# Float64 weights converted in pairs of chunks, with the low part formed on VectorE

## The chip, the cores and the metric

The kernel runs on one core of a Trainium2 chip. The metric is the time of one execution on the device, in microseconds (us); the median of several runs counts. The engines are TensorE (PE: matmuls, PEld: its weight loads), VectorE (DVE), ScalarE (ACT), GpSimd (POOL) and SyncE (SP), which issues all DMAs here. Each engine works through its own queue in order and waits at an instruction until what it needs is done.

## The reference

Attention with a window of 128 keys over 4 sequences of 576 tokens, 8 heads of 64, then two feed-forward networks (FFNs) over all 2304 tokens:

```python
scores = where(mask, scale * q @ k.T + bias, -1e9)      # causal, the last 128 keys
x = softmax(scores) @ v                                  # 2304 x 512
h = x @ w_in                                             # 512 -> 2048
x = (h * sigmoid(1.702 * h)) @ w_out                     # 2048 -> 512
g = x @ w_gate                                           # 512 -> 1536
out = (g * sigmoid(g) * (x @ w_val)) @ w_out2            # 1536 -> 512
```

q, k and v are float32. The five weight matrices are handed to the kernel as float64, and the kernel has to turn them into float32 itself.

## The kernel before

**Products.** Every float32 operand of an FFN product is split into hi + lo, two numbers of the type fp32r, and a product is three matmuls: hi by hi, hi by lo, lo by hi (`three`, L388 to L390). So weights, too, are needed as a hi and a lo part.

**Weights.** A chunk is 128 rows of 512 float64 numbers, 4 KB in each of the 128 partitions. The first FFN has 32 chunks (w_in and w_out in turn), the second 36 (w_gate, w_val, w_out2 in turn). `load_w` (L129) brings a chunk as pairs of 32-bit words into a slot of 4 KB; `split_w` (L135) turns it into float32 bit by bit and into hi and lo, which are written back into the same slot as the tile wt. It works in three steps. ScalarE rescales the upper words into the tile cv (L143). VectorE takes the sign (L145), joins it with the lower word's bits (L146) and joins both with the exponent and mantissa (L149). ScalarE copies the result to hi (L154), and GpSimd subtracts hi from it to make lo (L155). cv has three slots of one chunk.

**Slots.** The pool w has 32 slots, one for each chunk of the first FFN. Until a slot's chunk is loaded, block 0's queries, keys and values and the probabilities of blocks 0 and 1 lie in some of them (L95, L235, L236, L288, L312, L340). The second FFN's chunks come into four slots of their own (NX) and then into the slots of w in order, as the first FFN's last block has used the chunk in them.

**Order of work.** The first FFN and the attention go through the tokens in five blocks of 4, 3, 4, 3 and 4 tiles of 128 tokens. For each part f of the hidden layer, `h_part` makes the first product, ScalarE and VectorE apply the activation and the split into gh and gl (L409 to L414), and `y_part` makes the second product. `y_part` comes two parts after its `h_part` in the program (AHEAD). The attention of block 0 comes first, with an order written out by hand (`manual_schedule`, L555), into which the conversion of the first four chunks is put head by head (SPLITS0). The attention of the blocks after it lies in the gaps between the products of the block before. The order of the rest on each engine is set by a scheduler, which takes the program's order as priority, and which may run work earlier when its engine is free by its own estimate. So the first FFN's chunks are converted while block 0 goes through it, and the second FFN's while the last block does (L622 to L630). The second FFN goes through blocks of 4, 4, 4, 4 and 2 tiles, with `gv_part` and `o_part`; its split of the next block's input (L464) is on GpSimd.

**GpSimd's other work:** the probabilities' scaling (L269), the masks on transposed probabilities (L350, L353), and one of the two subtractions of a head's queries and keys (L204 for block 1, L208 for the others).

Of the kernel before, what the change touches and what calls it, by code (L numbers as in the profile page):

```python
# [8 lines left out]
F32 = mybir.dt.float32  # L9
F32R = mybir.dt.float32r  # L10
# [9 lines left out]
# how many parts of the hidden layers the first product of an FFN runs ahead of the second  # L20
AHEAD = 2
# parts of the first FFN's hidden layer that block 0 does before block 1, the rest after it
F0 = 10
# chunks of the second FFN's weights with slots of their own
NX = 4
# blocks of the first FFN and of the attention, in tiles of 128 tokens
A_BLOCKS = (4, 3, 4, 3, 4)
B_BLOCKS = (4, 4, 4, 4, 2)
# block 0's attention, in heads after a head's scores: its normalisation, transposes and values
NORM0, TRANSPOSE0, VALUES0 = 0.6, 2.2, 5.0  # L30
# heads of block 0 whose probabilities VectorE takes apart; ScalarE and GpSimd do the others
ON_VECTOR = (0, 2, 5)
# heads at which the splits of the first weight chunks begin, a head between their steps
SPLITS0 = (7, 8, 9, 10)
# the other blocks' attention: its share of the time, and lags in gaps between the FFN's products
SPREAD, SPLIT_LAG, TRANSPOSE_LAG, VALUES_LAG = 0.65, 0.3, 4.0, 3.0
# (1023 - 127) / 8 less in the upper eight bits of a float64's exponent
# [4 lines left out]
def attention_two_ffn(ctx: ExitStack, tc: tile.TileContext, q, k, v, w_in, w_out, w_gate, w_val, w_out2, yscr, out):  # L42
    """q, k: [H * D, tokens]; v: [H, 128, tiles, D]; w_in, w_gate, w_val: [F/128, 128, 512] and
    w_out, w_out2: [F, 512] as the bits of float64; yscr: [128, 4, tokens]; out: [tokens, 512].

    Every float32 operand of a product is split exactly into hi + lo with 12 significant
    bits each (float32r), so that single-pass products carry float32's accuracy."""
# [9 lines left out]
    NW1 = 2 * NF1  # L57
    NW2 = 3 * NF2
# [8 lines left out]
    # tiles of 128 tokens that go through the first and through the second FFN together, and,  # L67
    # for each block of the first, through the attention
# [6 lines left out]
    const = ctx.enter_context(tc.tile_pool(name="const", bufs=1))  # L75
    wpool = ctx.enter_context(tc.tile_pool(name="w", bufs=1, reuse_waits="tile"))
    cvp = ctx.enter_context(tc.tile_pool(name="cv", bufs=3))
# [13 lines left out]
    def constants():  # L91
        make_identity(nc, ident)
        # column j stands for the key at j in the query's tile up to the query's own position,
        # and beyond it for the key at j in the tile before: rel = key position - query position
        rel = wpool.tile([P, P], F32, tag=f"w{NW1 - 12}", name="rel")  # L95
        nc.gpsimd.iota(rel, pattern=[[1, P]], base=0, channel_multiplier=-1, allow_small_or_imprecise_dtypes=True)
        nc.vector.tensor_scalar(out=later, in0=rel, scalar1=0.0, scalar2=None, op0=ALU.is_gt)
        nc.vector.scalar_tensor_tensor(
            out=rel, in0=later, scalar=-float(WINDOW), in1=rel, op0=ALU.mult, op1=ALU.add
        )  # L100
        for h in range(H):
            # in units of unscaled scores
            slope = 2.0 ** (-8.0 * (h + 1) / H) / SCALE
            nc.vector.tensor_scalar(out=bias[:, h, :], in0=rel, scalar1=slope, scalar2=None, op0=ALU.mult)
        nc.vector.memset(never, -BIG)
        nc.vector.memset(drop, 1.0)
        nc.vector.memset(keep, 1.0)
# [21 lines left out]
    def load_w(pool, tag, src):  # L129
        """A chunk of float64 weights, as pairs of words, into the slot that its split will take."""  # L130
        t = pool.tile([P, 512, 2], U32, tag=tag, name="wraw")
        nc.sync.dma_start(out=t.rearrange("p c w -> p (c w)"), in_=src.bitcast(U32))
        return t, pool, tag

    def split_w(raw):  # L135
        """float64 -> float32 bit by bit (float32 has no exponents from 2^128, and those below 2^-119 go to zero),
        then hi + lo. In three steps."""
        words, pool, tag = raw
        low, high = words[:, :, 0], words[:, :, 1]
        c = cvp.tile([P, 512], U32, tag="cv", name="cv")  # L140
# [12 lines left out]
        t = pool.tile([P, 2, 512], F32R, tag=tag, name="wt")  # L153
        nc.scalar.activation(out=t[:, 0, :], in_=cf, func=AF.Copy)  # L154
        nc.gpsimd.tensor_tensor(out=t[:, 1, :], in0=cf, in1=t[:, 0, :].bitcast(F32), op=ALU.subtract)  # L155
        yield t

    def w1_src(i):
        f = i // 2
        return w_in[f] if i % 2 == 0 else w_out[f * P : (f + 1) * P, :]  # L160

    def w2_src(i):
        f = i // 3
        return (w_gate[f], w_val[f], w_out2[f * P : (f + 1) * P, :])[i % 3]

# [1 line left out]
    units = {}  # L167

    def span(j):
# [11 lines left out]
    def load_head(j, h):  # L181
        """Queries and keys, in both halves of the partitions."""
# [12 lines left out]
    def split_head(j, h):  # L195
        """Queries as hi over lo, keys as hi over hi and lo over lo: two products give all four parts."""
# [16 lines left out]
    def fold(i0, kinds, sb):  # L213
        """Puts the scores with the keys of the tile before into the places of the keys after the query."""
# [19 lines left out]
    # first slots of weights still to come that hold the probabilities of the first two blocks  # L234
    PROBS = (NW1 - 12, NW1 - 12)  # L235
    PFS = (NW1 - 20, NW1 - 8)  # L236
# [41 lines left out]
    def scores(j, h):  # L278
# [7 lines left out]
        else:  # L286
            if e == 0:
                u["probs"] = wpool.tile([P, 2, 4, P], F32, tag=f"w{PROBS[j] + h // 2}", name="probs")  # L288
            prob = u["probs"][:, e]
# [22 lines left out]
    def load_full(hp):  # L312
        """The first block's queries, keys and values, in slots of weights still to come: the queries of
        two heads, each head's keys with zeros in the other's place."""
        t0, n, _ = span(0)
        m = n * P
        qv = wpool.tile([P, 2, 512], F32, tag=f"w{NW1 - 8 + 2 * hp}", name="qv")
        kz = wpool.tile([P, 2, 512], F32, tag=f"w{NW1 - 7 + 2 * hp}", name="kz")
# [10 lines left out]
    def transposes(j, h):  # L329
        """A head's probabilities, keys on the partitions, apart by the tile of the key:  # L330
        before(0) own(0) before(1) own(1) ..."""
# [7 lines left out]
        else:  # L339
            pf = wpool.tile([P, 4, 2, P], F32, tag=f"w{PFS[j] + h}", name="pf")  # L340
# [3 lines left out]
        # of column q, partition k: the tile before for k > q, the query's own for k <= q  # L344
# [13 lines left out]
    def values(j, hp):  # L358
        """The outputs of two heads, which share TensorE's columns, by the tile of the keys."""
# [37 lines left out]
    def h_part(j, f):  # L397
# [3 lines left out]
        w = w1[2 * f]  # L401
# [6 lines left out]
        # x * sigmoid(1.702 x) = (1 + tanh(0.851 x)) * x / 2; the half is taken at the output  # L408
# [8 lines left out]
    def y_part(j, f):  # L417
# [7 lines left out]
        w = w1[2 * f + 1]  # L425
# [40 lines left out]
    def gv_part(b, f):  # L466
# [4 lines left out]
        for dst, w in ((pg, w2[3 * f]), (pv, w2[3 * f + 1])):  # L471
# [15 lines left out]
    def o_part(b, f):  # L487
# [4 lines left out]
        w = w2[3 * f + 2]  # L492
# [46 lines left out]
    load_w1(NW1 - 20)  # L539
# [18 lines left out]
    load_w1(8)  # L558
# [6 lines left out]
    def hooks(j, length):  # L565
        """The attention of block j, as (position, work) over the 2 * length gaps before its first FFN."""
# [37 lines left out]
    for idx, (j, f) in enumerate(seq):  # L604
        if (j, f) == (1, 0):
            load_w1(NW1)
        if j < 2:
            need = 2 * f + 3
            if j == 1:
                need = max(need, 2 * F0 + (2 * (NF1 - F0) * (f + 1)) // NF1)  # L610
# [11 lines left out]
        if j == na - 1:  # L622
            if f < KD:
                split_y(0, f, y2a)
            load_w2(NX if f == 0 else 2)
            split_next(w2, raw2, 2 * f - 4)
# [60 lines left out]
```

## Time and profile before

| | |
|---|---|
| median of 3 runs | 1008.58 us (1008.13 to 1009.61) |
| span of the profiled execution, first to last instruction | 1006.5 us |
| TensorE matmul busy | 964.8 us (96%) |
| VectorE busy | 528.1 us (52%) |
| ScalarE busy | 383.3 us (38%) |
| GpSimd busy | 265.2 us (26%) |
| bytes moved by DMA | 77.43 MB |

A row of the time line has an instruction's start, its length, the engine, the line of the kernel, the operation and its tiles (output<-input) with their shapes. A row of a group of instructions has their count (x), their busy time, the mean length of one in ns, and the idle time of the engine just before them. The rows of one engine overlap a little where the end of one is still under way as the next starts. Matmul ends are modelled, so TensorE's busy share says less than the number of its matmuls in a stretch.

### The profile page before, as it was taken

Reading aid. Unit: us, or ns where it says so; the run is one execution under the profiler, and the core shown is the slowest. Engines: PE = TensorE matmul, PEld = TensorE weight load, DVE = VectorE, ACT = ScalarE, POOL = GpSimd, SP = SyncE. Lnnn points to the kernel's source line nnn. Section 1 sums busy time; section 2 is a strip of 40 time slices with the busy share of each in tenths; the row PEclk is TensorE's granted clock in tenths of the full one; section 3 lists DMA queues with packets and bytes.
Section 4 is the critical chain, followed back from the end, with each engine's and each line's share of the span. In section 5 each row is a group of like instructions: output and inputs, shape, how many; then the busy total and the mean of one; then the engine's idle time right before and its main releaser. Section 6 shows DMA issues by size and latency. Waiting matters only on the chain.

```text
span 1006.5 us, 13342 instructions
## 1 busy us (share of the span) xinstructions
PE 964.8 (96%) x4792; PEld 804.3 (80%) x4792; DVE 528.1 (52%) x1138; ACT 383.3 (38%) x889; POOL 265.2 (26%) x327
## 2 busy tenths in 40 slices
PE   7887979999999999999888999999999999999998
PEld 5566669997878789998666788888888888888897
DVE  7899996564555345637999822232223222322232
ACT  4577753564444345635555521121121112111121
POOL 4756552363133125623444510100020001000000
PEclk9898999999999999999999999999999999999999
DMA  9824440132232113226444210010001000100010
GB/s 306 268 87 145 141 142 23 49 112 87 65 103 71 51 41 110 61 74 241 177 167 147 84 42 1 21 63 1 0 27 48 1 1 11 42 0 1 1 43 22
DMA packets 36579, 77.43 MB, mean 77 GB/s; under 512 B 5024, under 2 KB 13728, under 8 KB 36512
## 3 DMA queue, kind: packets, MB, share of 16 engines
q1 hardware_dynamic: 36512, 76.57, 23.3%
q8 instruction: 38, 0.62, 0.3%
q14 instruction: 29, 0.24, 0.1%
HBM read 66.06 MB, written 10.49 MB: 76 GB/s over the span
## 4 chain that ended last, share of the span: by engine, by line
PE 70%; DVE 18%; issue 4%; DMA 3%; ACT 2%; POOL 1%; SPq 0%; DVEq 0%; ACTq 0%; POOLq 0%
DVE wraw L146 6%; PE o L498 5%; PE o L496 5%; PE o L497 5%; DVE cv L149 5%; PE pg L388 5%; PE pg L390 5%; PE pv L388 5%; PE pv L390 5%; PE pg L389 5%; PE pv L389 5%; PE hp L388 4%; PE hp L389 4%; PE hp L390 4%; PE y L388 4%
## 5 line engine op out<-in xcount | busy, mean ns | idle before, releaser
L479 DVE SCALAR_TENSOR_TENSOR t<-t,pg 128x512 f32<-128x512 f32 (+1 forms) x60 | 38.0, 633 | 200.6 <-ACT t L478 200.6
L388 PE MATMUL hp<-xh,wt 128*128 128x512 f32 (+1 forms) x320 | 123.4, 386 | 8.5 <-DVE stat L241 3.1
L389 PE MATMUL y<-gl,wt 128*128 128x512 f32 (+1 forms) x320 | 120.2, 376 | 9.8 <-DVE gl L414 9.7
L155 POOL TENSOR_TENSOR wt<-cv,wt 128x512 fp32r<-128x512 f32 x68 | 98.7, 1453 | 113.0 <-ACT wt L154 113.0
L389 PE MATMUL hp<-xl,wt 128*128 128x512 f32 (+1 forms) x320 | 121.0, 378 | 2.0 <-DVE xl L383 2.0
L390 PE MATMUL hp<-xh,wt 128*128 128x512 f32 (+1 forms) x320 | 121.2, 379 | 0.1
L390 PE MATMUL y<-gh,wt 128*128 128x512 f32 (+1 forms) x320 | 118.8, 371 | 0.0
L388 PE MATMUL y<-gh,wt 128*128 128x512 f32 (+1 forms) x320 | 110.4, 376 | 4.5 <-ACT gh L413 4.5
L478 ACT ACTIVATE t<-pg 128x512 f32<-128x512 f32 (+1 forms) x60 | 33.2, 554 | 190.0 <-PE pg L390 190.0
L464 POOL TENSOR_TENSOR yl<-yr,yh 128x512 fp32r<-128x512 f32 (+1 forms) x20 | 24.8, 1252 | 268.5 <-ACT yh L463 268.5
L388 PE MATMUL pg<-yh,wt 128*128 128x512 f32 (+1 forms) x240 | 88.8, 370 | 0.0
L390 PE MATMUL pg<-yh,wt 128*128 128x512 f32 (+1 forms) x240 | 88.6, 369 | 0.0
L388 PE MATMUL pv<-yh,wt 128*128 128x512 f32 (+1 forms) x240 | 88.5, 369 | 0.0
L390 PE MATMUL pv<-yh,wt 128*128 128x512 f32 (+1 forms) x240 | 88.4, 368 | 0.0
L389 PE MATMUL pg<-yl,wt 128*128 128x512 f32 (+1 forms) x240 | 88.4, 368 | 0.0
L389 PE MATMUL pv<-yl,wt 128*128 128x512 f32 (+1 forms) x240 | 88.1, 367 | 0.0
L496 PE MATMUL o<-wt,p2h 128*128 128x512 f32 x216 | 84.7, 392 | 0.0
L498 PE MATMUL o<-wt,p2l 128*128 128x512 f32 x216 | 84.5, 392 | 0.2 <-DVE p2l L484 0.2
L497 PE MATMUL o<-wt,p2h 128*128 128x512 f32 x216 | 84.1, 390 | 0.0
L414 DVE TENSOR_TENSOR gl<-th,gh 128x512 fp32r<-128x512 f32 (+1 forms) x80 | 60.3, 754 | 44.0 <-ACT gh L413 42.9
L483 ACT ACTIVATE p2h<-t 128x512 fp32r<-128x512 f32 (+1 forms) x60 | 35.3, 588 | 124.0 <-DVE t L482 124.0
L388 PEld LDWEIGHTS hp<-xh,wt 128*128 128x128 f32 x320 | 62.1, 194 | 21.1 <-issue 5.5
(91 smaller groups left out, 1917.0 us busy)
## 6 DMA issues: line engine op xcount, KB each, us to landing
wraw<-in_moe_w_out SPq DMA_DIRECT2D x28, 512.0 KB, 4.7
wraw<-in_moe_w_in SPq DMA_DIRECT2D x16, 512.0 KB, 5.0
wraw<-in_moe_w_gate SPq DMA_DIRECT2D x12, 512.0 KB, 3.3
wraw<-in_moe_w_val SPq DMA_DIRECT2D x12, 512.0 KB, 3.2
kr<-in_k SPq DMA_DIRECT2D x32, 160.0 KB, 2.9
out<-ob SPq DMA_DIRECT2D x18, 256.0 KB, 2.1
kr<-in_k SPq DMA_DIRECT2D x32, 128.0 KB, 2.8
qr<-in_q SPq DMA_DIRECT2D x32, 128.0 KB, 2.8
```

The source lines that it names most:

```text
L146: nc.vector.scalar_tensor_tensor(out=low, in0=low, scalar=29, in1=high, op0=ALU.logical_shift_right, op1=ALU.bitwise_or)
L149: nc.vector.scalar_tensor_tensor(out=c, in0=c, scalar=3, in1=low, op0=ALU.logical_shift_left, op1=ALU.bitwise_or)
L155: nc.gpsimd.tensor_tensor(out=t[:, 1, :], in0=cf, in1=t[:, 0, :].bitcast(F32), op=ALU.subtract)
L388: nc.tensor.matmul(out=out_ap, lhsT=whi, rhs=xhi, start=start, stop=False)
L389: nc.tensor.matmul(out=out_ap, lhsT=whi, rhs=xlo, start=False, stop=False)
L390: nc.tensor.matmul(out=out_ap, lhsT=wlo, rhs=xhi, start=False, stop=stop)
L414: nc.vector.tensor_tensor(out=gl[:, :m], in0=th[:, :m], in1=gh[:, :m].bitcast(F32), op=ALU.subtract)
L479: nc.vector.scalar_tensor_tensor(out=th[:, :m], in0=th[:, :m], scalar=1.0, in1=pg[:, :m], op0=ALU.add, op1=ALU.mult)
L483: nc.scalar.activation(out=ph[:, :m], in_=th[:, :m], func=AF.Copy)
L496: nc.tensor.matmul(out=o, lhsT=ph[:, c], rhs=w[:, 0, :], start=(f == 0), stop=False)
L497: nc.tensor.matmul(out=o, lhsT=ph[:, c], rhs=w[:, 1, :], start=False, stop=False)
L498: nc.tensor.matmul(out=o, lhsT=pl[:, c], rhs=w[:, 0, :], start=False, stop=(f == NF2 - 1))
```

## The change

Two chunks are loaded into one slot of 8 KB and converted by instructions over both; `split_w` issues three VectorE instructions over 1024 columns for two chunks in place of six over 512, and ScalarE two in place of four. The last subtraction goes from GpSimd to VectorE, one over 1024 columns for a pair. The pool w has 16 slots of 8 KB instead of 32 of 4 KB, the second FFN's own slots are two instead of four, and cv has two slots of two chunks instead of three of one. A first FFN pair is w_in and w_out of the same part. The tenants of the weight slots move along: a slot holds four heads' probabilities instead of two, or q, k and v of a pair of heads in one slot instead of two. The conversions by hand are two, at heads 7 and 9, instead of four. Comments are gone; the other functions are the same but for the indices.

```diff
-NX = 4
+NX = 2
-SPLITS0 = (7, 8, 9, 10)
+SPLITS0 = (7, 9)
...
-    NW1 = 2 * NF1
-    NW2 = 3 * NF2
+    NW1 = NF1
+    NW2 = 3 * NF2 // 2
...
-    cvp = ctx.enter_context(tc.tile_pool(name="cv", bufs=3))
+    cvp = ctx.enter_context(tc.tile_pool(name="cv", bufs=2))
...
-    def load_w(pool, tag, src):
-        t = pool.tile([P, 512, 2], U32, tag=tag, name="wraw")
-        nc.sync.dma_start(out=t.rearrange("p c w -> p (c w)"), in_=src.bitcast(U32))
+    def load_w(pool, tag, srcs):
+        t = pool.tile([P, 2, 512, 2], U32, tag=tag, name="wraw")
+        for i, src in enumerate(srcs):
+            nc.sync.dma_start(out=t[:, i].rearrange("p c w -> p (c w)"), in_=src.bitcast(U32))
...
-        low, high = words[:, :, 0], words[:, :, 1]
-        c = cvp.tile([P, 512], U32, tag="cv", name="cv")
+        low, high = words[:, :, :, 0], words[:, :, :, 1]
+        c = cvp.tile([P, 2, 512], U32, tag="cv", name="cv")
...
-        t = pool.tile([P, 2, 512], F32R, tag=tag, name="wt")
-        nc.scalar.activation(out=t[:, 0, :], in_=cf, func=AF.Copy)
-        nc.gpsimd.tensor_tensor(out=t[:, 1, :], in0=cf, in1=t[:, 0, :].bitcast(F32), op=ALU.subtract)
-        yield t
+        t = pool.tile([P, 2, 2, 512], F32R, tag=tag, name="wt")
+        nc.scalar.activation(out=t[:, :, 0, :], in_=cf, func=AF.Copy)
+        nc.vector.tensor_tensor(out=t[:, :, 1, :], in0=cf, in1=t[:, :, 0, :].bitcast(F32), op=ALU.subtract)
+        yield [t[:, 0], t[:, 1]]
...
-            need = 2 * f + 3
+            need = f + 2
             if j == 1:
-                need = max(need, 2 * F0 + (2 * (NF1 - F0) * (f + 1)) // NF1)
+                need = max(need, F0 + (NF1 - F0) * (f + 1) // NF1)
...
-            load_w2(NX if f == 0 else 2)
-            split_next(w2, raw2, 2 * f - 4)
+            load_w2(NX if f == 0 else 1)
+            split_next(w2, raw2, f - 2)
```

## Rows read from the trace of the kernel before

**Rows 1.** The page's 40 slices of 25.2 us, busy tenths, TensorE's clock.

```profile
DVE  7899996564555345637999822232223222322232
...
PEclk9898999999999999999999999999999999999999
```

**Rows 2.** Three stretches: length, busy us (instructions) by engine, granted clock, DMA.

```profile
35.00:158.00 123.00, 104.44 (x491) 80.29 (x491) 120.69 (x233) 83.60 (x197) 72.71 (x62) 0.90 0.42 136
480.00:560.00 80.00, 69.65 (x291) 53.20 (x290) 79.36 (x99) 42.26 (x75) 35.58 (x26) 1.00 0.44 153
600.00:700.00 100.00, 100.00 (x438) 81.90 (x437) 26.61 (x39) 18.06 (x30) 5.59 (x4) 1.00 0.07 22
```

**Rows 3.** VectorE's time line, one turn of the second stretch.

```profile
507.79 0.67 DVE L410 SCALAR_TENSOR_TENSOR th<-th,hp 128x512 f32<-128x512 f32 x1
508.39 1.73 DVE L146 SCALAR_TENSOR_TENSOR wraw<-wraw 128x512 uint32<-128x512 uint32 x1
510.04 0.42 DVE L145 TENSOR_SCALAR wraw<-wraw 128x512 uint32<-128x512 uint32 x1
510.38 0.68 DVE L149 SCALAR_TENSOR_TENSOR cv<-cv,wraw 128x512 uint32<-128x512 uint32 x1
510.98 0.68 DVE L146 SCALAR_TENSOR_TENSOR wraw<-wraw 128x512 uint32<-128x512 uint32 x1
511.58 0.68 DVE L414 TENSOR_TENSOR gl<-th,gh 128x512 fp32r<-128x512 f32 x1
512.19 1.78 DVE L149 SCALAR_TENSOR_TENSOR cv<-cv,wraw 128x512 uint32<-128x512 uint32 x1
...
514.22 0.68 DVE L410 SCALAR_TENSOR_TENSOR th<-th,hp 128x512 f32<-128x512 f32 x1
```

**Rows 4.** GpSimd's time line in the same turn.

```profile
508.27 1.30 POOL L155 TENSOR_TENSOR wt<-cv,wt 128x512 fp32r<-128x512 f32 x1 [1.29 <-ACT wt L154]
511.80 1.61 POOL L155 TENSOR_TENSOR wt<-cv,wt 128x512 fp32r<-128x512 f32 x1 [2.23 <-ACT wt L154]
```

**Rows 5.** TensorE's waits, 480 to 560 us: total us, times, longest.

```profile
PE y L389 <- DVE gl L414: 9.7, 12, 1.5
```

**Rows 6.** VectorE's groups, 35 to 158 us: busy us, mean ns, idle before.

```profile
L146 DVE SCALAR_TENSOR_TENSOR wraw<-wraw 128x512 uint32<-128x512 uint32 x31 | 32.1, 1034 | 0.2
L149 DVE SCALAR_TENSOR_TENSOR cv<-cv,wraw 128x512 uint32<-128x512 uint32 x30 | 25.8, 860 | 0.5
L145 DVE TENSOR_SCALAR wraw<-wraw 128x512 uint32<-128x512 uint32 x32 | 21.7, 679 | 0.0
L414 DVE TENSOR_TENSOR gl<-th,gh 128x512 fp32r<-128x512 f32 x10 | 9.1, 906 | 0.0
...
L263 DVE TENSOR_SCALAR stat<-stat 128x3 f32<-128x3 f32 x8 | 6.7, 841 | 0.0
```

**Rows 7.** VectorE's time line, one L263 outside the first stretch.

```profile
33.81 0.17 DVE L263 TENSOR_SCALAR stat<-stat 128x4 f32<-128x4 f32 x1
```

**Rows 8.** GpSimd's groups with two inputs, 35 to 158 us.

```profile
L155 POOL TENSOR_TENSOR wt<-cv,wt 128x512 fp32r<-128x512 f32 x30 | 42.7, 1423 | 37.9 <-ACT wt L154 37.9
L204 POOL TENSOR_TENSOR kl<-kr,kh 128x512 fp32r<-128x512 f32 x8 | 12.3, 1532 | 5.2 <-ACT kh L203 5.1
```

**Rows 9.** Groups of L410 and L413 by shape, whole span.

```profile
L410 DVE SCALAR_TENSOR_TENSOR th<-th,hp 128x512 f32<-128x512 f32 x48 | 32.6, 679 | 22.0 <-ACT th L409 21.9
L413 ACT ACTIVATE gh<-th 128x512 fp32r<-128x512 f32 x48 | 30.0, 625 | 31.0 <-PE y L390 25.0 <-DVE th L410 6.0
...
L410 DVE SCALAR_TENSOR_TENSOR th<-th,hp 128x384 f32<-128x384 f32 x32 | 17.6, 549 | 16.1 <-ACT th L409 15.9
L413 ACT ACTIVATE gh<-th 128x384 fp32r<-128x384 f32 x32 | 16.6, 519 | 19.2 <-PE y L390 15.2 <-DVE th L410 4.0
```

**Rows 10.** ScalarE's time line in the turn of rows 3.

```profile
511.09 0.63 ACT L154 ACTIVATE wt<-cv 128x512 fp32r<-128x512 f32 x1 [1.80 <-DVE cv L149]
```

**Rows 11.** Waits of ScalarE for loads, 480 to 560 us.

```profile
ACT cv L143 <- DMA wraw<-in_moe_w_val: 2.1, 1, 2.1
```

More of the change, by code (lines that the diff above doesn't have):

```diff
@@ L81, in bank @@
         return ps.tile([P, 512], F32, tag="b", name=name)
+    QKV = NW1 - 4
+    PROBS = NW1 - 6
+    PFS = (NW1 - 10, NW1 - 4)
     ident = const.tile([P, P], F32, name="ident")
@@ L92, in constants @@
         make_identity(nc, ident)
-        rel = wpool.tile([P, P], F32, tag=f"w{NW1 - 12}", name="rel")
+        rel = wpool.tile([P, P], F32, tag=f"w{PROBS}", name="rel")
         nc.gpsimd.iota(rel, pattern=[[1, P]], base=0, channel_multiplier=-1, allow_small_or_imprecise_dtypes=True)
@@ L152, in split_w, with chunk @@
         yield
-        t = pool.tile([P, 2, 512], F32R, tag=tag, name="wt")
-        nc.scalar.activation(out=t[:, 0, :], in_=cf, func=AF.Copy)
-        nc.gpsimd.tensor_tensor(out=t[:, 1, :], in0=cf, in1=t[:, 0, :].bitcast(F32), op=ALU.subtract)
-        yield t
+        t = pool.tile([P, 2, 2, 512], F32R, tag=tag, name="wt")
+        nc.scalar.activation(out=t[:, :, 0, :], in_=cf, func=AF.Copy)
+        nc.vector.tensor_tensor(out=t[:, :, 1, :], in0=cf, in1=t[:, :, 0, :].bitcast(F32), op=ALU.subtract)
+        yield [t[:, 0], t[:, 1]]
     def w1_src(i):
-        f = i // 2
-        return w_in[f] if i % 2 == 0 else w_out[f * P : (f + 1) * P, :]
+        return w_in[i], w_out[i * P : (i + 1) * P, :]
     def w2_src(i):
-        f = i // 3
-        return (w_gate[f], w_val[f], w_out2[f * P : (f + 1) * P, :])[i % 3]
+        def chunk(c):
+            f = c // 3
+            return (w_gate[f], w_val[f], w_out2[f * P : (f + 1) * P, :])[c % 3]
+        return chunk(2 * i), chunk(2 * i + 1)
     units = {}
+    probs = {}
     def span(j):
@@ L232, in fold @@
             )
-    PROBS = (NW1 - 12, NW1 - 12)
-    PFS = (NW1 - 20, NW1 - 8)
     def softmax(j, h, n, sb, prob, stat):
@@ L286, in scores @@
         else:
-            if e == 0:
-                u["probs"] = wpool.tile([P, 2, 4, P], F32, tag=f"w{PROBS[j] + h // 2}", name="probs")
-            prob = u["probs"][:, e]
+            if h % 4 == 0:
+                probs[j] = wpool.tile([P, 4, 4, P], F32, tag=f"w{PROBS + h // 4}", name="probs")
+            prob = probs[j][:, h % 4]
         stat = att.tile([P, 4, TMAX], F32, tag="stat", name="stat", bufs=4)
@@ L316, in load_full @@
         m = n * P
-        qv = wpool.tile([P, 2, 512], F32, tag=f"w{NW1 - 8 + 2 * hp}", name="qv")
-        kz = wpool.tile([P, 2, 512], F32, tag=f"w{NW1 - 7 + 2 * hp}", name="kz")
+        qkv = wpool.tile([P, 4, 512], F32, tag=f"w{QKV + hp}", name="qkv")
+        qv, kz = qkv[:, :2], qkv[:, 2:]
         vs = qv[:, 1, : 2 * n * D].rearrange("p (e t d) -> p e t d", e=2, d=D)
@@ L339, in transposes @@
         else:
-            pf = wpool.tile([P, 4, 2, P], F32, tag=f"w{PFS[j] + h}", name="pf")
+            if h % 2 == 0:
+                u["pfs"] = wpool.tile([P, 2, 4, 2, P], F32, tag=f"w{PFS[j] + h // 2}", name="pf")
+            pf = u["pfs"][:, h % 2]
         before = pf[:, :n, 0, :]
@@ L400, in h_part @@
         xh, xl = xs[j]
-        w = w1[2 * f]
+        w = w1[f][0]
         for kk in range(KD):
@@ L424, in y_part @@
         gh, gl = gs.pop((j, f))
-        w = w1[2 * f + 1]
+        w = w1[f][1]
         for kk in range(KD):
@@ L470, in gv_part @@
         pv = bank("pv")
-        for dst, w in ((pg, w2[3 * f]), (pv, w2[3 * f + 1])):
+        for dst, c in ((pg, 3 * f), (pv, 3 * f + 1)):
+            w = w2[c // 2][c % 2]
             for kk in range(KD):
@@ L491, in o_part @@
         ph, pl = ps2.pop((b, f))
-        w = w2[3 * f + 2]
+        c = 3 * f + 2
+        w = w2[c // 2][c % 2]
         for i in range(n):
@@ L538, in attention_two_ffn @@
     constants()
-    load_w1(NW1 - 20)
+    load_w1(NW1 - 10)
     ev = []
@@ L557, in attention_two_ffn @@
             e()
-    load_w1(8)
+    load_w1(4)
     na = len(a_blocks)
```

## The prediction

> **What bounds the kernel now.** I read the page's slices first, then the table of stretches, then one turn of the loop engine by engine. The slices show where to look: VectorE is at nine tenths or more from 50 to 150 us (the first FFN's weights are converted under its block 0 and block 1's attention) and from 475 to 550 us (the second FFN's weights, under the first FFN's last block), and at two or three tenths in the second half [rows 1]. The stretches say what that costs [rows 2]. From 35 to 158 us VectorE is busy 120.7 of 123.0 us while TensorE, at a granted clock of 0.90, is busy 104.4. From 480 to 560 us VectorE is busy 79.4 of 80.0 and TensorE makes 291 matmuls, where an undisturbed stretch of the same matmuls makes 438 in 100 us, so 350 in 80: 59 matmuls of 0.228 us, 13.5 us, are lost. Elsewhere TensorE hardly rests, so the change can win in these two stretches alone.
>
> One turn of the second stretch shows why VectorE is full [rows 3]. From one L410 to the next are 6.43 us, in which two chunks are converted. Rows overlap by about 0.08 us, so I count from start to start: L145 0.34, L146, L149 and L414 0.60 each. L410 0.60 as well. By these a turn would be 2 x (0.34 + 0.60 + 0.60) + 2 x 0.60 = 4.3 us. The other 2.1 us are in two rows, an L146 of 1.73 us and an L149 of 1.78 us, each 1.05 to 1.10 above its twin of 0.68 in the same turn. GpSimd's two L155 rows lie exactly there [rows 4]: one runs from 508.27 to 509.57 and the long L146 ends 0.55 us later, the other ends at 513.41 and the long L149 0.56 us later, so each long row is a wait for GpSimd to end and then nearly its normal length. TensorE pays: its second product waits 9.7 us in 12 waits for gl of L414 [rows 5].
>
> In the first stretch the same excess stands in the group means [rows 6], against the short forms [rows 3, 7]: L146 31 x (1.034 - 0.68) = 11.0 us, L149 30 x 0.18 = 5.4, L145 32 x 0.26 = 8.3, L414 10 x 0.23 = 2.3, L263 8 x (0.84 - 0.17) = 5.4; 32.4 us together. Of GpSimd's two-input work L155 has 42.7 us beside 12.3 of L204 [rows 8], a share of 0.78. Since one-input GpSimd rows lie in the stretch too, I give L155 0.74 of the excess: 24 us, 0.80 us for each of its 30 chunks.
>
> **The change part by part.** *GpSimd's subtraction goes.* VectorE gets back 2 x 0.80 = 1.60 us a pair in the first stretch, and 2.1 us a turn in the second, where a turn holds one pair. GpSimd itself had time to spare in both.
>
> *The subtraction comes to VectorE.* It has the form of L414, two SBUF inputs. Its length for 1024 columns follows from the two lengths of L410 [rows 9]: 128 columns more cost 0.130 us, so 512 cost 0.53 and about 0.07 of the 0.60 is fixed. A row of 1024 takes 0.60 + 0.53 = 1.14 us, at most 1.20 if nothing is saved by pairing.
>
> *Three instructions for two chunks instead of six.* Each saves one fixed part: 3 x 0.07 = 0.21 us a pair, between 0 and that. After the change a pair needs 0.61 + 3 x 1.14 = 4.03 us of VectorE.
>
> *Stretch one:* -1.60 - 0.21 + 1.14 = -0.67 us a pair, x 15 pairs = -10.1 us. TensorE has room, since it is busy partly at the lower of its two clock levels (the slices' clock of 8 and 9 [rows 1]); VectorE's sum sets the end.
>
> *Stretch two:* VectorE needs 4.03 + 2 x 0.60 = 5.24 us a turn, TensorE 24 x 0.228 = 5.48. So TensorE would set the turn and 0.95 us of the 6.43 go; x 12 turns (the 12 waits of [rows 5]) = 11.4 us, and 13.5 at the most, the whole loss of TensorE.
>
> *A new wait.* The subtraction needs ScalarE's L154, and VectorE's queue is in order: behind it stand L410, L414 and block 1's softmax steps, and TensorE waits for those. Today the instruction that waits for L154 is on GpSimd, where nothing depends on the queue behind it. If the subtraction stands straight behind its L149, VectorE idles for the copy: L154 starts 0.03 us after L149's end and takes 0.63 us [rows 3, 10]. For the double form the two lengths of L413 give 0.109 us for 128 columns [rows 9], so 0.63 + 0.44 = 1.07 us; with the overlap and the handing over about 1.26 us a pair. If one instruction of 0.60 stands between, half of that; if L410 and L414 or the next pair's L145 and L146 stand there, nothing. The trace can't show the new order. It shows today's: in the turn each L146 is followed by the other chunk's L145 or by L414, not by its own chunk's L149 [rows 3], so the order interleaves what is ready. I take 0.2 us a pair; the ends are 0 and 1.26.
>
> *Coarser slots and loads.* A slot of 8 KB is loaded when both chunks in it have been used, so in the second stretch the first chunk's load starts a first-product later than now; its use in the second FFN is far off, but a late landing would hold ScalarE's L143, and VectorE behind it. Now such a wait is 2.1 us once in the stretch [rows 11]; I take no change, 0 to 3 us. The order on SyncE's queue stays, two transfers of 512 KB at a time. In the first stretch a first product waits for both chunks of its pair: one chunk's conversion, some 2 us, once, covered while VectorE still has the last split of block 0's values to do. The cv slots become two of a pair instead of three of a chunk, room for four chunks.
>
> *Longer rows in the way.* L410 and L414 now wait behind rows of 1.14 us instead of 0.60, and behind ScalarE rows of 1.07 instead of 0.63: at most 2 x 0.54 + 2 x 0.44 = 2.0 us more from a first product to its gl. The chain itself is about 2.6 us of such rows, and TensorE has another 5.48 us of products in between, so 4.6 us stay covered and the sum is unchanged. The Trainium skill (Perfetto Trace Analysis, Optimizing Scalar/DVE Operations) speaks against larger instructions in such a place: where VectorE isn't saturated but makes bubbles on others, breaking instructions up may help; by it the cover would be too small and the gain of stretch two would shrink. By the rows VectorE is saturated, so I leave it at zero.
>
> Sum: stretch one -10.1 + 15 x 0.2 = -7.1; stretch two 12 x (6.43 - max(5.48, 5.24 + 0.2)) = 11.4 less. Together -18.5 us. The profiled execution has a span of 1006.5 us against a median of 1008.6; the 2.1 us outside the span stay. 1008.6 - 18.5 = 990.
>
> **The rivals.** *No wait at all:* -10.1 - 13.5 gives 985; if the order also puts the last pairs' conversions behind block 1's products, where VectorE rests, some 7 us less again, 978. For it: the interleaving. *Half the copy is seen:* 0.63 us a pair leaves 15 x 0.04 = 0.6 us in the first stretch and a turn of 5.87, so 12 x 0.56 = 6.7 in the second: 1001. *VectorE waits for each copy (slower):* with 1.26 us a pair, the first stretch grows by 15 x 0.59 = 8.9 and a turn becomes 6.50, 0.8 more: 1018. It decides from a mean wait w with 15 x (w - 0.67) + 12 x (w - 1.19) = 0, that is 0.90 us a pair. For it: the second pass over cv needs the copy at once, and only two pairs are in hand; against it: L410 and L414 are two fillers a turn. *No relief:* the long rows come from something other than L155, and VectorE has 1.14 - 0.21 = 0.93 us a pair more: 15 x 0.93 + 12 x 0.93 = 25 us, 1034. The Trainium skill (the same page and section) has a rule that leads there: with a saturated VectorE, work may be given to GpSimd, though it adds that the two share a read port. Against it stand the ends of the long rows, 0.55 us behind both L155 rows.
>
> **How the numbers follow.** 0.2%, 2 us, is about what a measurement of this kernel can tell. Forecast 0.42, no wait or better 0.17, half the copy 0.20, within 2 us (waits near 0.90) 0.06, slower by the copy 0.12, no relief 0.03. Faster 0.79, same 0.06, slower 0.15. The range of 8 in 10 goes from 978 (the best order) to 1012 (a wait of 0.95 us, which costs 1.4, and 2 us of late loads); it leaves out most of the slower cases.
>
> **What would show it.** Right: no VectorE row of 1.7 us from 480 to 560 us, L146 and L149 at 1.2 us and the subtraction too, a turn of 5.5 us, TensorE without gaps there; the first stretch's end some 7 us earlier. Wrong: gaps on VectorE before the subtraction with ScalarE's L154 as releaser, near 1.2 us each; TensorE still waiting for gl; or L143 waiting for loads.

## The result: 989.6 us, and the profile after

The changed kernel takes 989.62 us (median of 4 runs, 989.23 to 990.62) where the kernel before takes 1008.43: a ratio of 0.9814, 95% interval [0.9801, 0.9828]. The span of its profiled execution is 988.0 us against 1006.5, so 18.5 us went. The prediction said 990 and 18.5 less. The sum is right, but it was reached by two errors that cancel: the first stretch gave 2.6 us where the sum had 7.1, the second about 15 where it had 11.4. That they cancel is luck.

The page of the changed kernel: engines' busy time, VectorE's slices and TensorE's clock (40 slices of 24.7 us), and the chain that ended last by engine.

```profile
PE 956.0 (97%) x4792; PEld 803.7 (81%) x4792; DVE 501.6 (51%) x1070; ACT 377.7 (38%) x821; POOL 167.1 (17%) x259
...
DVE  7799967574455436636999822232223222322232
...
PEclk9879999999999999999999999999999999999999
...
PE 89%; DVE 4%; DMA 3%; SPq 1%; ACT 1%; issue 1%; ACTq 0%; DVEq 0%
```

The stretches of [rows 2] in the changed kernel, same columns.

```profile
35.00:158.00 123.00, 103.92 (x505) 81.91 (x505) 106.16 (x200) 79.17 (x167) 30.43 (x32) 0.92 0.45 142
480.00:560.00 80.00, 80.00 (x353) 66.05 (x352) 77.24 (x89) 46.23 (x59) 2.43 (x2) 1.00 0.52 183
600.00:700.00 100.00, 100.00 (x439) 82.13 (x438) 26.28 (x38) 18.09 (x30) 5.59 (x4) 1.00 0.07 22
```

From 480 to 560 us TensorE is busy all 80.0 us with 353 matmuls; it had 69.65 and 291 [rows 2]. From 35 to 158 us VectorE is busy 106.2 us instead of 120.7, so 14.5 us of its time are free. TensorE is busy no longer than before there, 103.9 against 104.4.

A turn of the second stretch on VectorE, which answers to [rows 3] (L420 is th, L424 gl, L153, L154 and L157 the conversion, L163 the subtraction).

```profile
504.89 0.68 DVE L420 SCALAR_TENSOR_TENSOR th<-th,hp 128x512 f32<-128x512 f32 x1
505.48 1.22 DVE L157 SCALAR_TENSOR_TENSOR cv<-cv,wraw 128x1024 uint32<-128x1024 uint32 x1
506.62 0.69 DVE L153 TENSOR_SCALAR wraw<-wraw 128x1024 uint32<-128x1024 uint32 x1
507.22 0.69 DVE L424 TENSOR_TENSOR gl<-th,gh 128x512 fp32r<-128x512 f32 x1
507.82 1.22 DVE L154 SCALAR_TENSOR_TENSOR wraw<-wraw 128x1024 uint32<-128x1024 uint32 x1
508.96 1.22 DVE L163 TENSOR_TENSOR wt<-cv,wt 128x1024 fp32r<-128x1024 f32 x1
510.09 1.22 DVE L157 SCALAR_TENSOR_TENSOR cv<-cv,wraw 128x1024 uint32<-128x1024 uint32 x1
511.23 0.68 DVE L420 SCALAR_TENSOR_TENSOR th<-th,hp 128x512 f32<-128x512 f32 x1
...
515.63 0.68 DVE L420 SCALAR_TENSOR_TENSOR th<-th,hp 128x512 f32<-128x512 f32 x1
```

In this turn no row is above its short form. A row of 1024 of L154, L157 or L163 takes 1.22 us and 1.13 to 1.14 from start to start (L153 0.69 and 0.60), and the rows follow each other without a gap. Long and short turns alternate on VectorE now, here 6.34 us and then 4.40, 5.37 on the mean. Between a pair's L157 and its subtraction stand L424 and rows of the next pair.

**Where the 18.5 us went.** To see it by stretch, I take one landmark that every kernel has: the gl rows of the first FFN, 80 in each trace, always for the same pieces of work in the same order. "The gain at gl row n" is how much earlier than in the kernel before its n-th row starts. The 30th stands in the quiet part between the stretches. First the kernel before:

```profile
247.17 0.85 DVE L414 TENSOR_TENSOR gl<-th,gh 128x512 fp32r<-128x512 f32 x1 [0.88 <-ACT gh L413]
```

And the changed kernel:

```profile
244.61 0.84 DVE L424 TENSOR_TENSOR gl<-th,gh 128x512 fp32r<-128x512 f32 x1 [0.87 <-ACT gh L423]
```

So stretch one gave 2.6 us; from row 20 to row 34 the gain stays at 2.0 to 2.6. At row 64, before the second stretch, it is 3.0, and at the end 18.5: stretch two gave 15.5. About 0.5 of this is the landmark itself, which stands later on VectorE in the changed kernel; from row 60, where the gain is 3.5, to the end it is 15.0.

### The profile page after: what moved, and what is told of

It is laid out like the page before. It is cut to its first block, busy times and chain, and to the rows that moved or that the text cites. A ratio compares the mean times of both kernels' runs of the same rounds, so it can differ in the third digit from the quotient of the medians.

```text
span 988.0 us, 13012 instructions
## 1 busy us (share of the span) xinstructions
PE 956.0 (97%) x4792; PEld 803.7 (81%) x4792; DVE 501.6 (51%) x1070; ACT 377.7 (38%) x821; POOL 167.1 (17%) x259
## 4 chain that ended last, share of the span: by engine, by line
PE 89%; DVE 4%; DMA 3%; SPq 1%; ACT 1%; issue 1%; ACTq 0%; DVEq 0%
PE hp L398 6%; PE y L399 6%; PE y L400 6%; PE y L398 6%; PE hp L399 6%; PE hp L400 6%; PE pg L398 5%; PE o L508 5%; PE pg L400 5%; PE pv L398 5%; PE pv L400 5%; PE o L510 5%; PE pg L399 5%; PE pv L399 5%; PE o L509 5%; DMA wraw<-in_moe_w_out 3%
## 5 line engine op out<-in xcount | busy, mean ns | idle before, releaser
L398 PE MATMUL hp<-xh,wt 128*128 128x512 f32 (+1 forms) x320 | 120.9, 379 | 6.6 <-DVE cv L157 5.1
L399 PE MATMUL hp<-xl,wt 128*128 128x512 f32 (+1 forms) x320 | 119.0, 373 | 0.0
L400 PE MATMUL hp<-xh,wt 128*128 128x512 f32 (+1 forms) x320 | 118.9, 373 | 0.0
L474 POOL TENSOR_TENSOR yl<-yr,yh 128x512 fp32r<-128x512 f32 (+1 forms) x20 | 25.8, 1304 | 376.4 <-ACT yh L473 266.9
L424 DVE TENSOR_TENSOR gl<-th,gh 128x512 fp32r<-128x512 f32 (+1 forms) x80 | 56.3, 706 | 45.1 <-ACT gh L423 43.8
L420 DVE SCALAR_TENSOR_TENSOR th<-th,hp 128x512 f32<-128x512 f32 (+1 forms) x80 | 50.2, 630 | 44.5 <-ACT th L419 44.4
```

Of the source, the lines that this page charges most:

```text
L398: nc.tensor.matmul(out=out_ap, lhsT=whi, rhs=xhi, start=start, stop=False)
L399: nc.tensor.matmul(out=out_ap, lhsT=whi, rhs=xlo, start=False, stop=False)
L400: nc.tensor.matmul(out=out_ap, lhsT=wlo, rhs=xhi, start=False, stop=stop)
L420: nc.vector.scalar_tensor_tensor(out=th[:, :m], in0=th[:, :m], scalar=1.0, in1=hp[:, :m], op0=ALU.add, op1=ALU.mult)
L424: nc.vector.tensor_tensor(out=gl[:, :m], in0=th[:, :m], in1=gh[:, :m].bitcast(F32), op=ALU.subtract)
L474: nc.gpsimd.tensor_tensor(out=yl[:, kk, :m], in0=t[:, :m], in1=yh[:, kk, :m].bitcast(F32), op=ALU.subtract)
```

## Experiments

"Equal-work gain" in the expectations means the same thing as this gain, there read from TensorE's matmuls. Some matmul records are missing, and the gl rows are all there, so the measured gains below go by gl row 30 (stretch one) and by the end less gl row 64 (stretch two). Three runs whose instructions stand in exactly the same order gave 7.6, 8.3 and 9.4 in stretch one, so a difference below 2 us says nothing there. In the diffs "-" is the changed kernel unless another is named.

**pairs_on_gpsimd: the pairs without the move.**

```diff
-        nc.vector.tensor_tensor(out=t[:, :, 1, :], in0=cf, ...)
+        nc.gpsimd.tensor_tensor(out=t[:, :, 1, :], in0=cf, ...)
```

> The kernel after with one edit: the last subtraction, over a pair, is on GpSimd again. Theory (VectorE is held while GpSimd subtracts): GpSimd's row over 1024 columns takes about 2.5 us and VectorE has again one or two long rows a pair, some 2.0 us above their short form; a turn of the second stretch is 0.61 + 2 x 1.14 + 1.2 + 2.0 = 6.1 us against 5.45 after and 6.43 before, so 7 to 9 us of the second stretch come back; the first stretch is no better than after. In all 998 to 1008 us. Rival (larger instructions bring the gain, the place of the subtraction little): no long rows, under 993 us.

Measured: 1017.49 us, ratio 1.0082 [1.0066, 1.0097], slower than the kernel before and than the theory's range: stretch one -4.6, stretch two -3.8. Two rows of VectorE, 480 to 560 us, and the GpSimd row beside the second:

```profile
505.94 2.39 POOL L163 TENSOR_TENSOR wt<-cv,wt 128x1024 fp32r<-128x1024 f32 x1 [4.80 <-ACT wt L162]
```

```profile
502.22 1.21 DVE L154 SCALAR_TENSOR_TENSOR wraw<-wraw 128x1024 uint32<-128x1024 uint32 x1
...
506.01 3.41 DVE L154 SCALAR_TENSOR_TENSOR wraw<-wraw 128x1024 uint32<-128x1024 uint32 x1
```

The GpSimd row ends at 508.33, the long L154 1.09 us later: a wait, and then nearly the normal length. The Trainium skill (SBUF — State Buffer, Who interferes with whom) says that a VectorE instruction with two inputs in SBUF contends with a GpSimd instruction that reads SBUF, and that the port pair they share is an exclusive lock; this row agrees. The long rows aren't all of the loss: from 480 to 560 us VectorE also stands idle for ScalarE's rescaling of the next pair, which the theory hadn't named.

```profile
DVE wraw L153 <- ACT cv L151: 12.5, 7, 3.3
```

Pairs without the move win nothing.

**chunks_on_vector: the move without the pairs** (one line of the kernel before).

```diff
-        nc.gpsimd.tensor_tensor(out=t[:, 1, :], in0=cf, ...)
+        nc.vector.tensor_tensor(out=t[:, 1, :], in0=cf, ...)
```

> The kernel before with one edit: the last subtraction, over one chunk, is on VectorE. Theory (the relief is the place of the subtraction): a turn of the second stretch needs 2 x (0.34 + 3 x 0.60) + 1.2 = 5.5 us of VectorE, as much as TensorE's 5.45, so most of the second stretch's 14.9 us is won, 11 to 14 us; the first stretch, without the coarse start, gains 3 to 7 us. In all 988 to 995 us, no more than 5 us from the kernel after and perhaps faster. Rival (pairs are needed, since the fixed part of six instructions instead of three fills VectorE): second stretch under 8 us, total over 998 us.

Measured: 984.02 us, ratio 0.9758 [0.9732, 0.9785]: faster than the changed kernel, and than the 988 to 995 expected. Stretch two +14.9, about as with pairs; stretch one +7.6, 5 us more than with them. Its VectorE is busy longer in stretch one, not shorter:

```profile
35.00:158.00 123.00, 107.44 (x534) 86.08 (x535) 118.26 (x269) 85.59 (x202) 33.03 (x32) 0.93 0.46 142
```

118.3 us of VectorE here against 106.2 in the changed kernel, and TensorE makes 534 matmuls against 505. So the pairs save VectorE 12 us in this stretch and the kernel with them is 5 us behind at its end.

**start_by_chunks: is it the late second pair?** In the changed kernel TensorE stands 5.09 us ahead of its product at 54.04. Here the first two pairs come as four single chunks.

```diff
-SPLITS0 = (7, 9)
+SPLITS0 = (7, 8, 9, 10)
...
+        if tag in ("w0", "w1"):
+            ... # two slots of 4 KB, each chunk loaded and converted by itself
```

> The kernel after, with the first two pairs of the first FFN (and the two pairs of the second FFN that follow in their slots) loaded and converted by single chunks, at heads 7, 8, 9 and 10 as in the kernel before. Theory (the first stretch gains only 2.6 us because the second pair is ready at 54 us and TensorE stands 5.1 us before it): that wait is gone, TensorE is 5 to 8 us further at 62 us, and the total falls by 2 to 6 us against after, to 984 to 988 us. Rival (VectorE's sum alone sets the end of the stretch, so an earlier start is given back by 121 us): within 1.5 us of after, 988 to 991 us.

Measured: 992.1 us, ratio 0.9838 [0.9823, 0.9853]; stretch one -0.8, stretch two +15.1. TensorE's gaps from 45 to 65 us:

```profile
50.20 0.50 PE L425 MATMUL hp<-xh,wt 128*128 128x512 f32 x1 [2.37 <-ACT wt L189]
...
61.19 0.79 PE L425 MATMUL hp<-xh,wt 128*128 128x512 f32 x1 [4.99 <-ACT wt L169]
```

The theory fell, and the time is above the rival's too: the gap moved to the third pair.

**need_later, chunks_earlier, chunks_later: the requested lead.** The code asks, ahead of each part of the first FFN, for so many converted chunks.

```diff
-            need = f + 2
+            need = f + 1          # need_later
```

```diff
-            need = 2 * f + 3      # chunks_on_vector
+            need = 2 * f + 4      # chunks_earlier
+            need = 2 * f + 2      # chunks_later
```

> The changed kernel with one number altered: in the first FFN a part f asks for f + 1 converted pairs before its products instead of f + 2, so that the tenth part asks for 20 chunks where the changed kernel asks for 22 and the kernel before for 21; instructions, slots and loads stay. Theory, that the pairs lose stretch one because VectorE converts one chunk more ahead of need while TensorE waits for it: two chunks of about 1.9 us each no longer lie ahead of the products, the equal-work gain at the end of stretch one rises from 2.6 to about 6 us, and the run takes 985 to 987 us. Rival, that the unit itself costs the time (a product waits for the whole pair, a row of 1024 elements stands before a short one): the gain of stretch one stays at 2.6 us or falls, 989 to 994 us.

> The kernel before with the last subtraction on VectorE (single chunks, 984.0 us) and one number altered: a part f asks for 2f + 4 converted chunks instead of 2f + 3, which is what the pairs ask for; no pair, no larger slot, no longer row in it. Theory, order ahead of need: one chunk more, about 1.9 us, lies ahead of the products in stretch one; 985.5 to 987 us, equal-work gain of stretch one 4 to 5 us instead of 6.5. Rival, that the pair as a unit costs the time: nothing changes, 983 to 985 us.

> The same kernel of single chunks with 2f + 2 instead of 2f + 3. Theory, order ahead of need: one chunk less, about 1.9 us, lies ahead of the products in stretch one: 981 to 983 us. Rival: no change, 983 to 985 us; or, if a chunk then comes too late for its product, slower, 985 to 990 us with new waits of TensorE for a converted chunk between 40 and 110 us.

Measured: need_later 989.48 us [0.9787, 0.9823], chunks_earlier 984.66 [0.9741, 0.9790], chunks_later 983.44 [0.9727, 0.9760]. None differs from its parent, and none could: in all three the instructions of every engine stand in the same order as in the parent, so the request changed nothing. These runs say nothing on the theory. They are repeats, and give the spread named above (2.6 and 1.2; 7.6, 8.3 and 9.4 us in stretch one). The two spare runs at the end of this section keep the changed kernel's order on VectorE too, and gave 0.8 and 2.8.

**first_by_halves: is it the long row?** Each pair of the first FFN is converted with instructions of 512, one chunk behind the other; slots and order by pairs stay.

```diff
+        for i in range(2):
+            ... c[:, i], high and low of words[:, i]   # every step of split_w, 512 wide
```

> The changed kernel (slots of two chunks, the order by pairs) in which every pair of the first FFN is converted with two instructions of 512 elements a row in place of one of 1024, the two halves of a step one behind the other. The fixed part of an instruction comes back (0.21 us for a pair by the sum of the prediction, some 2 us over the ten pairs that lie ahead), the long row goes. Theory, order ahead of need: as the changed kernel or a little slower, 989 to 992 us. Rival, that the length of a row or the wait for the copy of a whole pair costs stretch one its gain: 984 to 987 us.

Measured: 996.79 us, ratio 0.9875 [0.9856, 0.9893]; stretch one -4.0, stretch two +15.6. Slower than both expectations: stretch one is 6.6 us behind the changed kernel's. Nothing here shows the long rows to be a loss; but the order of VectorE's rows changed with the edit, so what the rows alone are worth isn't shown. The Trainium skill (Perfetto Trace Analysis, Optimizing Scalar/DVE Operations) says that where VectorE isn't saturated but makes bubbles on other engines, breaking instructions up may let work be completed sooner; in this stretch, where VectorE is busy 106.2 of 123.0 us in the changed kernel, it was completed later.

**chunks_four_slots, chunks_two_slots, pairs_one_slot: how far VectorE can run ahead.** The working tile cv bounds how many chunks are under way: three with single chunks, four (two pairs) in the changed kernel.

```diff
-    cvp = ... name="cv", bufs=3      # chunks_on_vector
+    cvp = ... name="cv", bufs=4      # chunks_four_slots
+    ... two tiles for the first FFN, three for the second   # chunks_two_slots
```

```diff
-    cvp = ... name="cv", bufs=2
+    ... one tile for the first FFN, two for the second      # pairs_one_slot
```

> The kernel before with the last subtraction on VectorE (single chunks, 984.0 us) and four working tiles cv of one chunk instead of three; the changed kernel's two tiles of a pair hold four chunks too. No pair and no longer row in it, but VectorE's order changes: ahead of the fifth to eighth th rows of the first FFN stand 13, 17, 19 and 21 converted chunks (12, 14, 17 and 18 with three tiles; 16, 18, 20 and 20 in the changed kernel). Theory, that the pairs lose stretch one by conversions ahead of need: two to three chunks of 1.9 us each lie ahead of the products, the equal-work gain at the end of stretch one falls from 6.5 to 2 to 4 us, 986 to 989 us. Rival, that the pair as a unit costs the time (a product waits for both chunks and for the copy of both): no change, 983 to 985 us.

> The kernel of single chunks with the subtraction on VectorE (984.0 us) and two working tiles cv instead of three for the first FFN (the second keeps three). Ahead of the fifth to eighth th rows stand 10, 14, 15 and 17 chunks instead of 12, 14, 17 and 18. Theory, order ahead of need: one chunk less lies ahead, stretch one gains 1 to 2 us more, 981.5 to 983.5 us. Rival: no change, 983 to 985 us, or slower, up to 990 us, if a chunk's first copy then waits for a subtraction and a product for the chunk.

> The changed kernel with one working tile cv of a pair for the first FFN instead of two (the second FFN keeps two). Ahead of the fifth to eighth th rows stand 10, 14, 16 and 16 converted chunks instead of 16, 18, 20 and 20, so the conversions come nearer to their need; the price is that a pair's first copy waits until the subtraction of the pair before has ended. Theory, order ahead of need: the equal-work gain at the end of stretch one rises from 2.6 to 5 to 7 us, 985 to 988 us. Rival, the pair as a unit: nothing is won, and the serial chain of a pair (a copy of 1.13 us, three rows of 0.6 to 1.14, a copy, a row of 1.14) shows as new waits, 990 to 996 us.

Measured:

| kernel | us | ratio | stretch one | stretch two | VectorE busy 35-120 / 120-158 us | clock 35-120 |
|---|---|---|---|---|---|---|
| single, two tiles | 981.87 | [0.9725, 0.9751] | +9.9 | +15.3 | 80.7 / 36.7 | 0.90 |
| single, three | 984.02 | [0.9732, 0.9785] | +7.6 | +14.9 | 81.4 / 36.8 | 0.90 |
| single, four | 997.27 | [0.9883, 0.9914] | -8.2 | +15.2 | 79.1 / 29.6 | 0.84 |
| pairs, one | 989.24 | [0.9790, 0.9819] | +2.7 | +15.4 | 72.8 / 30.9 | 0.86 |
| pairs, two (the change) | 989.62 | [0.9801, 0.9828] | +2.6 | +15.5 | 80.5 / 25.6 | 0.88 |

With single chunks one more tile costs 13 us by the medians, without a pair or a long row in the kernel; the theory had 2 to 5. (The two traces are 16 us apart: that of four tiles is from the slowest of its five runs, 1000.6 us.) Two windows of the kernel with four tiles:

```profile
35.00:120.00 85.00, 61.72 (x267) 46.18 (x268) 79.13 (x187) 55.78 (x134) 23.45 (x25) 0.84 0.40 125
120.00:158.00 38.00, 35.36 (x188) 27.50 (x186) 29.62 (x64) 24.41 (x57) 4.87 (x7) 1.00 0.51 172
```

And of the kernel with two:

```profile
35.00:120.00 85.00, 70.61 (x341) 53.93 (x342) 80.69 (x198) 61.44 (x157) 27.94 (x30) 0.90 0.50 149
120.00:158.00 38.00, 38.00 (x209) 34.89 (x209) 36.70 (x69) 25.00 (x46) 2.37 (x2) 1.00 0.36 121
```

With four tiles VectorE is as full up to 120 us, but TensorE makes 267 matmuls instead of 341, and then VectorE has 8.4 us of idle time. The reading is that conversions came first and the rows that TensorE waited for later. The changed kernel has the same mark, 25.6 of 38 us. TensorE's gaps with four tiles, and what follows one:

```profile
54.72 0.79 PE L388 MATMUL hp<-xh,wt 128*128 128x512 f32 x1 [5.99 <-DVE stat L263]
...
69.18 2.08 PE L388 MATMUL y<-gh,wt 128*128 128x512 f32 x4 [4.42 <-ACT gh L413]
...
111.21 1.06 PE L336 MATMUL pt<-ident,probs 128*128 128x128 f32 x3 [3.75 <-ACT probs L267]
...
113.14 0.63 PE L389 MATMUL hp<-xl,wt 128*128 128x512 f32 x1
113.57 0.63 PE L390 MATMUL hp<-xh,wt 128*128 128x512 f32 x1
```

With pairs, one tile won nothing. The wait only changed its name, as the rival said, though the time stayed that of the changed kernel. TensorE's largest wait from 35 to 120 us with one tile:

```profile
PE hp L398 <- ACT wt L162: 14.4, 5, 6.2
```

Against the same single chunks, two tiles win 1.6 to 2.8 us in the median over the three kernels with three tiles. But the intervals of the ratios overlap, and stretch one alone (+9.9 against 7.6 to 9.4) is within the spread, so this isn't shown to be a win. It is the lowest median I have: one instruction on another engine and one working tile less for the first FFN.

**spare_two_inputs, spare_one_input: the contention priced alone.** The changed kernel with one GpSimd row more for each pair of the second FFN, whose result nothing uses.

```diff
+        if extra:   # second FFN only
+            spare = bias...
+            nc.gpsimd.tensor_tensor(out=spare, in0=cf[:, 0], in1=cf[:, 1], op=ALU.subtract)   # two inputs
+            nc.gpsimd.tensor_copy(out=spare, in_=cf[:, 0])                                     # one input
```

> The kernel after, with one more GpSimd instruction for each pair of the second FFN: it subtracts one half of cv from the other and writes to memory that nobody reads. No data waits for it but the slot of cv. Theory (GpSimd's two-input row holds VectorE whatever it computes): its row takes 1.3 to 1.6 us, in most of the 18 pairs a VectorE row is 0.9 to 1.1 us longer, a turn is 6.2 to 6.4 us instead of 5.45, and the second stretch loses 8 to 14 us: 998 to 1004 us. Rival (the long rows before came from waits of data, not from GpSimd being busy): no long rows, within 2 us of after.

> The changed kernel with a spare GpSimd copy of 512 elements a row for each pair of the second FFN; it reads one operand from SBUF (one of the pair's two converted chunks) where the spare subtraction of the earlier run read two, and its result is used by nothing. That earlier run took 997.9 us, 8 more than the changed kernel. Theory, that what holds a VectorE row is a GpSimd row with two operands from SBUF: 989 to 991.5 us, no VectorE rows of 1.5 us and more beside the copies between 480 and 560 us. Rival, that any GpSimd row which reads SBUF holds it: 994 to 998 us.

Measured: two inputs 997.88 us (one run), stretch two +8.8 instead of 15.5; one input 989.68 us, ratio 0.9815 [0.9802, 0.9829], stretch two +15.1. Two inputs, GpSimd and then VectorE:

```profile
513.88 1.62 POOL L163 TENSOR_TENSOR bias<-cv 128x512 f32<-128x512 f32 x1 [5.30 <-DVE cv L157]
```

```profile
513.66 0.68 DVE L153 TENSOR_SCALAR wraw<-wraw 128x1024 uint32<-128x1024 uint32 x1
514.26 1.79 DVE L427 TENSOR_TENSOR gl<-th,gh 128x512 fp32r<-128x512 f32 x1
```

One input:

```profile
508.11 0.95 POOL L163 COPY bias<-cv 128x512 f32<-128x512 f32 x1 [5.28 <-DVE cv L157]
```

```profile
508.50 1.10 DVE L427 TENSOR_TENSOR gl<-th,gh 128x512 fp32r<-128x512 f32 x1
```

Two inputs hold VectorE 1.1 us here, and 0.8 in the next turn (an L153 of 1.48 us): a turn of 5.24 us by the sum's terms plus about 0.95 is more than TensorE's 5.48, and stretch two loses 6.7 us. (The run is 8 us slower in all; the rest lies in stretch one, where the edit adds nothing, within the spread there.) VectorE's rows stand in the same order in both spare kernels as in the changed one, so this difference isn't one of order. The theory that the copy holds nothing fell, though its time came; the rival's mechanism was right and its time wrong. The copy holds L427 for 0.42 us, until it has ended, and in the other turn an L153 for 0.1. That is some 0.26 us a turn, which about fits into what VectorE has to spare.

## Why the prediction was right, and where it was not

**VectorE was the bound, by GpSimd's subtraction** [rows 2 to 4]: right for stretch two. Pairs with the subtraction on GpSimd won nothing, with it on VectorE every form of the kernel won; one spare row with two inputs took back 6.7 of the 15.5 us of stretch two. The rival "no relief" (1034) is out.

**The row of 1024, 1.14 us, and three instructions for six** [rows 9]: right. The rows stand 1.13 to 1.14 us apart.

**The new wait, taken at 0.2 us a pair:** right in kind, lower in size. From 480 to 560 us VectorE waited three times for the copy, 1.0 us over 15 subtractions, 0.07 us a pair; from 35 to 158 us twice, 1.4 us over 14, 0.1 a pair. L420 or L424 and rows of the next pair fill the place, as the argument for the interleaving had it. The rivals "half the copy" (1001) and "each copy" (1018) fell with that.

**Stretch two, 12 x 0.95 = 11.4, cap 13.5:** mechanism right, the waits priced too low. TensorE makes the turn now, as forecast. Measured: 15.5 us here (15.0 from row 60), and 14.9 to 15.6 in every kernel with the subtraction on VectorE and no spare row of two inputs. The sum gave each of the twelve waits what a middle turn loses. TensorE's rows in the kernel before show that the first and the last but one are longer:

```profile
484.69 0.39 PE L388 MATMUL y<-gh,wt 128*128 128x512 f32 x1
486.61 0.50 PE L389 MATMUL y<-gl,wt 128*128 128x512 f32 x1 [1.53 <-DVE gl L414]
486.95 0.40 PE L390 MATMUL y<-gh,wt 128*128 128x512 f32 x1
...
493.04 0.50 PE L389 MATMUL y<-gl,wt 128*128 128x512 f32 x1 [0.70 <-DVE gl L414]
...
550.87 0.50 PE L389 MATMUL y<-gl,wt 128*128 128x512 f32 x1 [1.54 <-DVE gl L414]
```

The wait at 486.61 takes 1.92 us from the start of the matmul before and 0.34 to the one after, where 0.228 is usual: 1.80 us lost. The one at 550.87 loses 1.8 too, each of the nine from 493.04 on about 0.94, the last, at 557.28, 0.88; a wait for gh at 547.89 loses 0.86. Together 13.8, which is the cap but for 0.3; the remaining 1.2 of the 15.0 are 0.5 at a wait at 573.59, behind the stretch, and small differences that I don't follow further. Ahead of 486.61 TensorE doesn't wait, though VectorE has long rows there already (a gl row of 1.36 us at 471.38 us). Same columns as in [rows 2]:

```profile
440.00:480.00 40.00, 40.00 (x196) 35.47 (x197) 26.29 (x37) 18.67 (x33) 14.56 (x10) 1.00 0.62 215
```

**Stretch one, -7.1:** this is the step that failed, at "VectorE's sum sets the end". VectorE's relief came, even above the forecast (14.5 us less busy, where the sum had 10.1 less the waits). TensorE got 2.6 of it; its waits did not shrink: the idle times ahead of its rows from 35 to 158 us add up to 18.4 us before and 18.7 in the changed kernel (18.7 to 21.2 in the four traces with that order on VectorE). With single chunks and three tiles they are 14.7 to 15.9, with four tiles 25.8. Two sentences of the prediction bear on it. One is that "a first product waits for both chunks of its pair: one chunk's conversion, some 2 us, once, covered". In the changed kernel TensorE stands 5.09 us for a product that needs a pair, so it wasn't covered, and 3.59 us for gl.

```profile
54.04 0.80 PE L398 MATMUL hp<-xh,wt 128*128 128x512 f32 x1 [5.09 <-DVE cv L157]
...
70.65 0.79 PE L399 MATMUL y<-gl,wt 128*128 128x512 f32 x1 [3.59 <-DVE gl L424]
```

But this wait doesn't set the pairs apart: with single chunks on VectorE TensorE has one as long at nearly the same place, behind another row.

```profile
51.03 0.80 PE L388 MATMUL hp<-xh,wt 128*128 128x512 f32 x1 [4.98 <-DVE stat L263]
```

The other names the room of four chunks in cv and gives it no price. Single chunks show that this room alone can cost 13 us. The reading that fits is that VectorE's order puts conversions ahead of what TensorE waits for, and that the time saved comes back as idle time of VectorE at the end of the stretch. VectorE's rows of the changed kernel at that point:

```profile
126.48 0.69 DVE L420 SCALAR_TENSOR_TENSOR th<-th,hp 128x512 f32<-128x512 f32 x1 [1.21 <-ACT th L419]
128.49 0.69 DVE L424 TENSOR_TENSOR gl<-th,gh 128x512 fp32r<-128x512 f32 x1 [1.32 <-ACT gh L423]
129.10 0.55 DVE L393 TENSOR_TENSOR xl<-xb,xh 128x384 fp32r<-128x384 f32 x1
134.99 0.69 DVE L420 SCALAR_TENSOR_TENSOR th<-th,hp 128x512 f32<-128x512 f32 x1 [5.34 <-ACT th L419]
```

**Longer rows in the way, taken at 0:** no loss shown. Broken up, the same pairs lose 6.6 us in stretch one, more than the 0.21 us a pair of the sum would give over its 15 pairs (3.2), so another order probably has a part in it.

**Coarser loads, 0 to 3 us:** late landings did come. ScalarE waited for weights ten times from 480 to 560 us (7.9, 5.6 and 4.0 us for the three tensors, where [rows 11] had 2.1 once), but TensorE shows no gap, so they cost nothing.

**What stays open.** Why the pairs are 5 us behind single chunks in stretch one. That a depth of four costs time is shown for single chunks, by one edit. For pairs it is a reading, not shown: a pair allows four chunks under way or two, and with two the chain of one pair becomes the wait. The lead by itself doesn't rank the kernels: counted by the L149 and L157 rows of the traces, 14, 18, 20 and 22 chunks stand ahead of the fifth to eighth th row in the changed kernel and in that of four tiles alike, and they gained +2.6 and -8.2. Each edit of depth, start or row length also changes the whole order. No run held the order still and changed the unit alone.

## What to carry to other kernels

When two engines hold each other up, price the move by itself: one instruction moved gave 24 to 25 us here, and the larger units that came with it gave 5 to 6 back. Relief of a full engine is a gain only for the rows that the bound engine waits for; look where its queue spends the freed time, and treat the number of working tiles as a setting of that order, where one more can cost time (13 us here). And price the waits of the bound engine one by one, from start to start: a middle turn's loss times their number missed the longer ones.

## What the runs showed of the hardware beyond that

A GpSimd row that reads one operand holds VectorE too, until it has ended: 0.42 us of a copy of 0.95, against 1.1 of a subtraction of 1.62. The held rows here were a gl row with both inputs in SBUF and an L153 with one.

TensorE's idle time cost more than itself in one place. In the kernel with four tiles the granted clock is 1.00 ahead of the gap of 3.75 us that ends at 111.21 us, and 0.50 behind it, so it fell from the higher of the two levels (2.4 GHz) to the lower (1.2 GHz):

```profile
106.00:107.40 1.40, 1.40 (x10) 1.13 (x8) 1.40 (x5) 0.97 (x2) 0.00 (x0) 1.00 0.26 75
112.00:116.00 4.00, 3.73 (x9) 2.78 (x9) 3.93 (x11) 2.98 (x10) 1.25 (x2) 0.50 0.46 135
```

Matmuls of 512 columns start 0.43 us apart there (113.14 to 113.57 in the rows shown above) where 0.228 is usual. The ten from 112.55 to 116.91 us take 4.36 us instead of 2.28, so about 2 us come on top of the gap. From 35 to 120 us the clock is 0.84 with four tiles and 0.90 with two or three, so this is part of why one more tile cost 13 us and not the 2 to 5 of the theory.
